# Where the FFT units stand in the slot list of a fused FFT filter and squared-ReLU feed-forward kernel

## The chip, the cores and the metric

The kernel runs on one core of one Trainium2 chip. The metric is device time in microseconds (us) of one execution. All times below come from the runs of the kernel before the change and from one profiled execution of it.

## What is computed

The input is x of shape 8 x 3008 x 256 (batch, sequence, channel). Along the sequence each channel goes through a real FFT, is multiplied by a complex filter and comes back through the inverse FFT. The result, read as 24064 rows of 256, goes through a feed-forward layer with a squared ReLU.

```python
X = np.fft.rfft(x, axis=1)
Y = X * (filt_r + 1j * filt_i)[None, :, :]
y = np.fft.irfft(Y, n=x.shape[1], axis=1)
h = np.maximum(y.reshape(24064, 256) @ w_in, 0.0)     # w_in 256 x 2048
out = h * h @ w_out                                   # w_out 2048 x 256
```

## The kernel before

**The feed-forward part sets the beat.** The rows are taken in 47 groups of 512. Each group has eight slots, so slot s belongs to group s // 8. In a slot TensorE (PE) makes two 128 x 512 blocks of h out of `yt` and the first weights (`ffn_g1`, L553). ScalarE (ACT) applies the ReLU (L557), and VectorE (DVE) squares the blocks of two slots at once (L564). One group later PE multiplies the squares with the second weights. For groups 0 to 5 and the last one that is `ffn_g2` (L573). For groups 6 to 45 it is `products` (L666), a scheme with seven products of half-size blocks instead of eight. That scheme needs four sums of h blocks (`sums`, DVE, L639 to L648) and adds on DVE (L681, L687) ahead of the stores (L604, L606) to `out`. The stores are issued by SyncE (SP). A `top` and a `bot` half are stored for each group, and the pool of their tiles has three buffers.

**The FFT part is cut into units that are strewn between.** The length 3008 is 64 x 47, and a batch goes through four stages:

- `load_x` (GpSimd's DMA queue, POOL) brings x, and `unit_a` (L358, 16 per batch) does the 47-point stage. ACT or DVE copies its result out of PSUM (L362, L364). After each four units `write_u` writes 384 KB to a DRAM tensor `dU`.
- `read_u` reads `dU` back in another order, with one 512 KB DMA and one 1024 KB DMA (L433), into the single buffer `ut`. `unit_b` (L442, 12 per batch) does the 64-point stage. DVE multiplies the result by the filter straight out of PSUM (L450), and two POOL DMAs add the two halves of the product to each other (L457). The products have five buffers. The first four units of a batch need the 512 KB part alone.
- `unit_p` (L487, 12 per batch) does the inverse 64-point stage on the finished product. ACT copies it out (L489), and after each three units 384 KB are written to `dZ` (L492).
- `read_z` reads a quarter of `dZ` with two 192 KB DMAs (L505) into one of two tiles `zt`, which the quarters use in turn. `unit_y` (L523, 16 per batch, four per quarter) does the inverse 47-point stage and ACT or DVE puts it into `yt` (L530, L532). `ffn_g1` reads `yt`. The first four units of a batch must be done before the group that holds the batch's first rows.

All units of the four kinds write to one PSUM tag with two buffers (`psF`). A unit can start when the copy out of the unit before the last has ended.

**The order is written out by hand.** Each engine works through its instructions in the order of the program, and so does SP's queue of DMA issues. `fft_plan(b)` (L690) gives each unit and each read of batch b a place counted in half-slots from a first slot `f` of the batch, which is 48 slots ahead of the group in which its rows begin (40 for batch 1). So batch b's list starts at slot 40, 88, 136, 184, 232 and 280 for b = 2 to 7. `run` (L729) executes what stands at a half-slot: place 0 comes right after the slot's `ffn_g1`, place 1 after its `products` or `ffn_g2`. The lists of all batches are merged into one dictionary, and nothing keeps two units out of the same half-slot. From f on, batch b still has its products to make while batch b + 1 has its `unit_a`. From f + 39 on, the first things of b + 1 and the `unit_y` of b stand among each other. This stretch, slots f + 38 to f + 55, is called the boundary of batch b in what follows.

Of the kernel before, what the change touches and what calls it, by code (L numbers as in the profile page):

```python
# [19 lines left out]
TG = 512  # L20
SLOTS = 8
# [89 lines left out]
def kernel(  # L111
# [9 lines left out]
    nc = tc.nc  # L121
    B, S, D = x.shape
# [564 lines left out]
                nc.vector.tensor_add(out=v, in0=o, in1=v)  # L687
                store(g, 0, 2, f["top"])

    def fft_plan(b):  # L690

        plan = {}

        def put(r, f, *a):
            r = int(2 * r)
            plan.setdefault(divmod(r, 2), []).append((f, a))

        d = 0
        if b == 1:
            for n in range(4, 16):  # L700
                put((n if n < 8 else n + 2 if n < 12 else 2 * n - 7) + n % 2 / 2, unit_y, 0, n)
            put(7.5, read_z, 0, 3)
            for k in range(4):
                put((4.5, 5.5, 7.5, 7.5)[k], cast_wout, k, nc.vector)
            for a in range(12, 16):
                put(2 + a / 2, unit_a, b, a)
            put(10.5, read_u, b)
            d = 7
        else:
            for a in range(16):  # L710
                if a % 2 == 0 and b > 2:
                    put((-57 + 2.3 * a) if b == 3 else (-66 + 2.75 * a), load_x, b, a // 2)
                put((-16 + a, -46 + 2.2 * a, -56 + 2.75 * a)[min(b, 4) - 2], unit_a, b, a)
            put(2 if b == 2 else -9, read_u, b)
        for p in range(12):
            r = 14 + 15 * p / 11 if b == 1 else 6 + 28 * p / 11 if b == 2 else -5 + 39 * p / 11
            put(r, unit_b, b, p)
            if b == 1 and 2 <= p < 10:
                put(r, load_x, 2, p - 2)
            put(r + 4.5, unit_p, b, p)  # L720
        for c in range(4):
            put((41, 41.5, 48, 54)[c] - d, read_z, b, c)
        for n in range(16):
            put(YN[n] - d, unit_y, b, n)
        return plan

    YN = (45, 45.5, 46, 46.5, 47.5, 49, 50.5, 52, 54, 56, 58, 60, 63, 66, 69, 72)

    def run(plan, r, place):  # L729
        for f, a in plan.get((r, place), ()):  # L730
            f(*a)


# [8 lines left out]
    for k in range(2):  # L742
        c = slice(12 * k, 12 * k + 12)
# [26 lines left out]
    for k in range(6):  # L770
        if k % 3 == 0:
            sSPx.append(p_u.tile([128, 12, 128], F16, tag="u", name=f"sSPx_{k}"))
        c, o = slice(4 * k, 4 * k + 4), slice(4 * k % 12, 4 * k % 12 + 4)
# [27 lines left out]
    read_z(0, 2)  # L801

    SEVEN = range(6, NG - 1)
    work = {}
    for b in range(1, B):
        first = (b * S // TG) * SLOTS - (48 if b > 1 else 40)
        for (r, place), w in fft_plan(b).items():
            work.setdefault((first + r, place), []).extend(w)

    for s in range((NG + 1) * SLOTS):  # L810
        g, k = divmod(s, SLOTS)
        if g < NG:
            ffn_g1(g, k)
        run(work, s, 0)
        if SEVEN[0] * SLOTS <= s < SEVEN[0] * SLOTS + 4:
            make_t(s % SLOTS)
        if (s - 1) // SLOTS - 1 in SEVEN:
            products((s - 1) // SLOTS - 1, (s - 1) % SLOTS)
        if g > 0 and g - 1 not in SEVEN:
            ffn_g2(g - 1, k)  # L820
        run(work, s, 1)
        if g > 0 and g - 1 not in SEVEN:
            ffn_out(g - 1, k)
        if g - 1 in SEVEN:
            sums(g - 1, k)
        if g < NG:
            ffn_sq(g, k)
# [30 lines left out]
```

## Time and profile before

| | |
|---|---|
| median of 14 runs | 788.09 us (785.9 to 790.35) |
| the profiled execution | 786.35 us, its span 784.2 us |
| TensorE busy | 754.8 us, 96% of the span, at full granted clock |
| VectorE busy | 619.7 us, 79% |
| ScalarE busy | 583.3 us, 74% |
| GpSimd busy | 192.7 us, 25% |
| DMA | 109.21 MB, mean 139 GB/s |

The page gives one execution. Busy time is the time in which an engine has an instruction in work. For TensorE the ends of matmuls are modelled, and a matmul is in work for longer than it keeps the next one from starting. A wait is put down to the line and the engine that ended it. An issue on SP's queue is not a transfer: the row tells when the DMA was handed over, not when it landed.

### The profile page before, as it was taken

The numbers are of one execution on the slowest core, as the hardware profiler recorded it, in microseconds if no ns is written. First come the engines' busy times: TensorE is split into PE (matmuls) and PEld (weight loads), VectorE is DVE, ScalarE is ACT, GpSimd is POOL, SyncE is SP. The second block draws the span as 40 slices with busy tenths as digits, with TensorE's granted clock in tenths as the row PEclk, the third lists the DMA queues.
The fourth block names the chain that finished last, engine by engine and source line by source line (L and its number), as shares of the span: only waits on it lengthen the run. The fifth ranks groups of instructions, "written<-read, shape, count | busy, mean of one in ns | idle before, by whom it ended". The sixth has DMA issues, their size and how long they took to land.

```text
span 784.2 us, 19161 instructions
## 1 busy us (share of the span) xinstructions
PE 754.8 (96%) x8022; PEld 553.2 (71%) x8022; DVE 619.7 (79%) x679; ACT 583.3 (74%) x831; POOL 192.7 (25%) x260
## 2 busy tenths in 40 slices
PE   8989989999989999999999999999998999999998
PEld 6746656667767777777768777687776877777776
DVE  5856654579778988888987899779987999878874
ACT  3976777778877887778877887778786777777774
POOL 3801650134213321222221323233311222000000
PEclk9999999999999999999999999999999999999999
DMA  9985896655775547665486554855536433421011
GB/s 364 373 252 159 151 169 190 168 105 116 148 195 127 108 99 183 165 129 99 106 217 131 113 125 97 207 128 116 103 87 193 121 69 80 112 70 55 28 50 60
DMA packets 104942, 109.21 MB, mean 139 GB/s; under 512 B 9640, under 2 KB 93096, under 8 KB 102936
## 3 DMA queue, kind: packets, MB, share of 16 engines
q1 hardware_dynamic: 85704, 87.38, 36.3%
q0 software_dynamic: 19008, 20.43, 19.6%
q8 instruction: 63, 1.03, 0.6%
q10 hardware_dynamic: 144, 0.18, 0.1%
q14 instruction: 23, 0.19, 0.1%
HBM read 58.12 MB, written 48.23 MB: 136 GB/s over the span
## 4 chain that ended last, share of the span: by engine, by line
PE 80%; DMA 9%; DVE 6%; ACT 2%; SPq 2%; issue 1%; DVEq 0%; ACTq 0%
PE psH L553 35%; PE psX L666 16%; PE psY L666 12%; PE psO L573 6%; DMA zt<-dZ 4%; DVE prod L450 3%; PE psA L358 3%; PE psP L487 2%; PE psY L523 2%; PE psB L442 2%; DMA f<-in_filt_i_dram 2%; DVE h L564 1%; DMA ut<-dU 1%; ACT h L557 1%; DMA wout<-in_moe_w_out_dram 1%
## 5 line engine op out<-in xcount | busy, mean ns | idle before, releaser
L557 ACT ACTIVATE h<-psH 128x1024 f16<-128x1024 f32 x376 | 384.6, 1024 | 156.6 <-PE psH L553 152.6
L553 PE MATMUL psH<-yt,sWin 128*128 128x512 f16 (+7 forms) x1728 | 386.7, 351 | 1.5 <-DVE yt L532 0.6
L564 DVE TENSOR_TENSOR h<-h 128x2048 f16<-128x2048 f16 (+1 forms) x192 | 229.8, 1197 | 68.5 <-ACT h L557 64.9
L457 POOL DMA_DIRECT2D prod<-prod x168 | 138.8, 972 | 462.3 <-DVE prod L450 456.4
L553 PEld LDWEIGHTS <-sWin 128*128 128x128 f16 x1728 | 152.8, 98 | 97.0 <-issue 3.8
L666 PEld LDWEIGHTS <-sum 128*128 128x128 f16 x2560 | 158.0, 98 | 25.2 <-issue 1.5
L666 PEld LDWEIGHTS <-h 128*128 128x128 f16 x1920 | 119.0, 98 | 20.5 <-issue 1.4
L450 DVE TENSOR_TENSOR prod<-psB,sF 128x1024 f16<-128x1024 f32 x84 | 102.5, 1220 | 26.6 <-PE psB L442 26.3
L666 PE MATMUL psX<-sT,sum 128*128 128x128 f16 x1280 | 91.0, 219 | 0.0
L666 PE MATMUL psY<-sT,sum 128*128 128x128 f16 x640 | 61.9, 219 | 0.0
L573 PE MATMUL psO<-sWout,h 128*128 128x256 f16 x448 | 56.9, 272 | 0.0
L523 PEld LDWEIGHTS <-zt 112*128 112x128 f16 x512 | 34.1, 98 | 29.2 <-issue 8.4
L532 DVE CAST yt<-psY 128x376 f16<-128x376 f32 x62 | 33.7, 544 | 26.1 <-PE psY L523 26.0
L362 ACT CAST u<-psA 96x512 f16<-96x512 f32 x90 | 52.3, 581 | 2.5 <-PE psA L358 1.9
L573 PEld LDWEIGHTS <-h 128*128 128x128 f16 x448 | 43.2, 98 | 14.8 <-issue 4.5
L489 ACT CAST ze<-psP 128x512 f16<-128x512 f32 x84 | 49.3, 587 | 4.1 <-PE psP L487 3.9
L523 PE MATMUL psY<-sC,zt 112*128 112x94 f16 x512 | 42.4, 205 | 9.5 <-DMA zt<-dZ 9.3
L642 DVE TENSOR_TENSOR sum<-sum,h 128x2048 f16<-128x2048 f16 x40 | 48.9, 1222 | 0.9
L666 PE MATMUL psY<-sWout,h 128*128 128x128 f16 x640 | 48.8, 219 | 0.0
L666 PE MATMUL psX<-sT,h 128*128 128x128 f16 x640 | 48.8, 219 | 0.0
L648 DVE TENSOR_TENSOR sum<-h,sum 128x2048 f16<-128x2048 f16 x40 | 48.6, 1216 | 0.0
L666 PE MATMUL psY<-sWout,sum 128*128 128x128 f16 x640 | 48.6, 219 | 0.0
(86 smaller groups left out, 706.1 us busy)
## 6 DMA issues: line engine op xcount, KB each, us to landing
zt<-dZ SPq DMA_DIRECT2D x64, 192.0 KB
dU<-u SPq DMA_DIRECT2D x28, 384.0 KB
prod<-prod POOLq DMA_DIRECT2D x168, 64.0 KB, 2.8
dZ<-ze SPq DMA_DIRECT2D x28, 384.0 KB
x<-in_x_dram POOLq DMA_DIRECT2D x40, 192.0 KB, 4.7
ut<-dU SPq DMA_DIRECT2D x7, 1024.0 KB
xw<-in_x_dram SPq DMA_DIRECT2D x6, 1024.0 KB
ut<-dU SPq DMA_DIRECT2D x7, 512.0 KB
```

The lines of the kernel that those rows point to most:

```text
L362: nc.scalar.copy(out=o, in_=pv)
L450: nc.vector.tensor_mul(out=prod, in0=ps.rearrange("p (a d) -> p a d", d=D).unsqueeze(1).to_broadcast([128, 2, 2, D]), in1=sF[:, :, 2 * p:2 ...
L457: nc.gpsimd.dma_start(out=prod[64 * i:64 * i + 64, 0], in_=prod[64 - 64 * i:128 - 64 * i, 1], accum_op=mybir.AluOpType.add)
L489: nc.scalar.copy(out=zes[(b, c)][:, 2 * i6:2 * i6 + 2, :], in_=ps.rearrange("p (a d) -> p a d", d=D))
L523: nc.tensor.matmul(ps[:, 94 * jj:94 * jj + 94], zt[:, 4 * (g % 2) + jj, dt * 128:(dt + 1) * 128], sSY, start=True, stop=True)
L553: nc.tensor.matmul(ps[:, i, o:o + n], sWin[:, dt, jt * 128:(jt + 1) * 128], yts[b][:, dt, r:r + n], start=(dt == 0), stop=(dt == 1))
L557: nc.scalar.activation(out=h2[:, 2 * s:2 * s + 2, :], in_=ps, func=AF.Relu)
L564: nc.vector.tensor_mul(out=v, in0=v, in1=v)
L573: nc.tensor.matmul(pso[g][:, t % 2, :], h2s[g][:, jt, t * 128:(t + 1) * 128], sWout[:, jt, :], start=(jt == 0), stop=(jt == NJT - 1))
L642: nc.vector.tensor_sub(out=t, in0=f[5], in1=a11)
L648: nc.vector.tensor_sub(out=t, in0=a12, in1=f[6])
L666: nc.tensor.matmul(o[:, t, :], f[p][:, q, 128 * t:128 * t + 128], sg["w"][p][:, q, :], start=(m == 0 and p in (1, 2)), stop=(q == 7), skip ...
```

## The change

Units no longer share half-slots. `fft_plan` now makes one list for all batches. Units of batch 1, and the first four `unit_y` of every batch, keep fixed places. All others have a wished place, and go, kind by kind (`unit_b`, `unit_p`, `unit_y`, `unit_a`), to the nearest half-slot that is still free. A half-slot with more than two of its four neighbours taken counts as two half-slots further away. Reads and loads are placed as before, and may share a half-slot with a unit.

Places that change, in slots after f:

- The first quarter of `dZ` is read at 40 instead of 41, and the second at 43 instead of 41.5. The reads of the third and fourth quarter stay at 48 and 54.
- `read_u` of the next batch goes from 9 to 6.5 slots ahead of that batch's f. For batches 3 to 7 that is from f + 39 of the batch before to f + 41.5: it was ahead of the first read of `dZ` and is now behind it. Batch 2's `read_u` stays where it is.
- The 12 `unit_b` of batches 3 to 7 go over 36 slots from -2 instead of 39 slots from -5.
- For batches 2 to 7 `unit_p` stands 7 slots behind its `unit_b` for the first one, falling to 4.5 for the last, instead of 4.5 throughout.
- `unit_y` 4 to 7 stand half a slot later (48, 49.5, 51, 52.5), and batch 3's `unit_a` are 2.1 slots apart instead of 2.2.

No instruction, DMA or tile is added or taken away. In the new list, units of batch 1 still share a half-slot with another unit at slots 19.5, 23.5 and 29.

```diff
-    def fft_plan(b):
-
-        plan = {}
-
-        def put(r, f, *a):
-            r = int(2 * r)
-            plan.setdefault(divmod(r, 2), []).append((f, a))
...
-                put((-16 + a, -46 + 2.2 * a, -56 + 2.75 * a)[min(b, 4) - 2], unit_a, b, a)
-            put(2 if b == 2 else -9, read_u, b)
-        for p in range(12):
-            r = 14 + 15 * p / 11 if b == 1 else 6 + 28 * p / 11 if b == 2 else -5 + 39 * p / 11
-            put(r, unit_b, b, p)
-            if b == 1 and 2 <= p < 10:
-                put(r, load_x, 2, p - 2)
-            put(r + 4.5, unit_p, b, p)
-        for c in range(4):
-            put((41, 41.5, 48, 54)[c] - d, read_z, b, c)
-        for n in range(16):
-            put(YN[n] - d, unit_y, b, n)
-        return plan
-
-    YN = (45, 45.5, 46, 46.5, 47.5, 49, 50.5, 52, 54, 56, 58, 60, 63, 66, 69, 72)
+    YN = (45, 45.5, 46, 46.5, 48, 49.5, 51, 52.5, 54, 56, 58, 60, 63, 66, 69, 72)
+
+    def fft_plan():
+
+        fixed, units, moves = [], [], []
+        for b in range(1, B):
+            f = (b * S // TG) * SLOTS - (48 if b > 1 else 40)
...
+                    units.append((f + (-16 + a, -46 + 2.1 * a, -56 + 2.75 * a)[min(b, 4) - 2],
+                                  unit_a, b, a))
+                moves.append((f + (2 if b == 2 else -6.5), read_u, b))
+            for p in range(12):
+                r = 14 + 15 * p / 11 if b == 1 else 6 + 28 * p / 11 if b == 2 else -2 + 36 * p / 11
+                (fixed if b == 1 else units).append((f + r, unit_b, b, p))
+                if b == 1 and 2 <= p < 10:
+                    moves.append((f + r, load_x, 2, p - 2))
+                (fixed if b == 1 else units).append((f + r + (4.5 if b == 1 else 7 - 2.5 * p / 11), unit_p, b, p))
+            for c in range(4):
+                moves.append((f + (40 + d / 7, 43, 48, 54)[c] - d, read_z, b, c))
+            for n in range(16):
+                (fixed if n < 4 else units).append((f + YN[n] - d, unit_y, b, n))
+        work, used, done = {}, set(), {}
+        for r, *u in fixed:
+            h = int(2 * r)
+            used.add(h)
+            work.setdefault(h, []).append(u)
+        rank = (unit_b, unit_p, unit_y, unit_a)
+        for r, *u in sorted(units, key=lambda u: (rank.index(u[1]), u[0])):
+            after = done.get((u[0], u[1]), -1)
+            h = min((h for h in range(max(int(2 * r) - 3, after + 1), int(2 * r) + 12)
+                     if h not in used),
+                    key=lambda h: (sum(h + i in used for i in (-2, -1, 1, 2)) > 2) * 2
+                    + abs(h - int(2 * r)))
+            used.add(h)
+            done[(u[0], u[1])] = h
+            work.setdefault(h, []).append(u)
+        for r, *u in moves:
+            work.setdefault(int(2 * r), []).append(u)
+        return work
+
+    def run(plan, s, place):
+        for f, *a in plan.get(2 * s + place, ()):
             f(*a)
...
-    work = {}
-    for b in range(1, B):
-        first = (b * S // TG) * SLOTS - (48 if b > 1 else 40)
-        for (r, place), w in fft_plan(b).items():
-            work.setdefault((first + r, place), []).extend(w)
+    work = fft_plan()
```

More of the change, by code (lines that the diff above doesn't have):

```diff
@@ L688, in products @@
                 store(g, 0, 2, f["top"])
-    def fft_plan(b):
-        plan = {}
-        def put(r, f, *a):
-            r = int(2 * r)
-            plan.setdefault(divmod(r, 2), []).append((f, a))
[L698 to L712, printed above, removed]
-                put((-16 + a, -46 + 2.2 * a, -56 + 2.75 * a)[min(b, 4) - 2], unit_a, b, a)
-            put(2 if b == 2 else -9, read_u, b)
-        for p in range(12):
-            r = 14 + 15 * p / 11 if b == 1 else 6 + 28 * p / 11 if b == 2 else -5 + 39 * p / 11
-            put(r, unit_b, b, p)
-            if b == 1 and 2 <= p < 10:
-                put(r, load_x, 2, p - 2)
-            put(r + 4.5, unit_p, b, p)
-        for c in range(4):
-            put((41, 41.5, 48, 54)[c] - d, read_z, b, c)
-        for n in range(16):
-            put(YN[n] - d, unit_y, b, n)
-        return plan
@@ L727 @@
-    YN = (45, 45.5, 46, 46.5, 47.5, 49, 50.5, 52, 54, 56, 58, 60, 63, 66, 69, 72)
-    def run(plan, r, place):
-        for f, a in plan.get((r, place), ()):
+    YN = (45, 45.5, 46, 46.5, 48, 49.5, 51, 52.5, 54, 56, 58, 60, 63, 66, 69, 72)
[3 more added lines that the diff above has]
+            f = (b * S // TG) * SLOTS - (48 if b > 1 else 40)
+            d = 0
+            if b == 1:
+                for n in range(4, 16):
+                    fixed.append(((n if n < 8 else n + 2 if n < 12 else 2 * n - 7) + n % 2 / 2,
+                                  unit_y, 0, n))
+                moves.append((7.5, read_z, 0, 3))
+                for k in range(4):
+                    moves.append(((4.5, 5.5, 7.5, 7.5)[k], cast_wout, k, nc.vector))
+                for a in range(12, 16):
+                    fixed.append((2 + a / 2, unit_a, b, a))
+                moves.append((10.5, read_u, b))
+                d = 7
+            else:
+                for a in range(16):
+                    if a % 2 == 0 and b > 2:
+                        moves.append((f + ((-57 + 2.3 * a) if b == 3 else (-66 + 2.75 * a)),
+                                      load_x, b, a // 2))
+                    units.append((f + (-16 + a, -46 + 2.1 * a, -56 + 2.75 * a)[min(b, 4) - 2],
[29 more added lines that the diff above has]
+        return work
```

## Prediction, made before the result was known

> **What bounds the kernel now.** I read the page first: the busy times, and the chain of work that ended last.
>
> ```profile
> PE 754.8 (96%) x8022; PEld 553.2 (71%) x8022; DVE 619.7 (79%) x679; ACT 583.3 (74%) x831; POOL 192.7 (25%) x260
> PE 80%; DMA 9%; DVE 6%; ACT 2%; SPq 2%; issue 1%; DVEq 0%; ACTq 0%
> ```
>
> PE is the bound, and no matmul leaves the program. All that can be won is PE's idle time and what is lost with it. So I cut the trace along the batches. The columns are the stretch, its length, and PE busy (instructions) first.
>
> ```profile
> 212.80:247.30 34.50, 31.54 (x380) 24.17 (x378) 27.22 (x30) 25.38 (x39) 7.70 (x10) 1.00 0.71 174
> 307.10:340.90 33.80, 31.58 (x380) 25.05 (x378) 27.23 (x30) 25.42 (x39) 7.71 (x10) 1.00 0.70 176
> 340.90:400.70 59.80, 59.80 (x653) 43.17 (x649) 52.35 (x56) 48.14 (x71) 16.42 (x22) 1.00 0.54 114
> 400.70:434.80 34.10, 31.58 (x380) 25.56 (x378) 27.22 (x30) 25.42 (x39) 7.70 (x10) 1.00 0.72 174
> 494.60:528.50 33.90, 31.57 (x380) 25.06 (x378) 27.22 (x30) 25.41 (x39) 8.93 (x12) 1.00 0.71 175
> 588.30:620.10 31.80, 29.75 (x373) 23.40 (x371) 27.06 (x30) 22.37 (x33) 6.57 (x8) 1.00 0.60 160
> ```
>
> Five short stretches, the boundaries of batches 2 to 6, lose 34.50 - 31.54 = 2.96, then 2.22, 2.52, 2.33 and 2.05 us: 12.1 in all. The long stretch between two of them loses nothing. It holds 32 slots, 1.87 us each. Then PE's waits, from 200 to 640 us and from 95 to 200 us; the columns are the sum, the number and the longest.
>
> ```profile
> PE psY L523 <- DMA zt<-dZ: 7.8, 5, 2.0
> PE psP L487 <- DVE prod L450: 2.4, 5, 0.5
> PE psA L358 <- DVE prod L450: 1.9, 8, 0.3
> ```
>
> ```profile
> PE psA L358 <- ACT ze L489: 1.5, 2, 1.2
> PE psA L358 <- ACT yt L530: 1.1, 1, 1.1
> PE psA L358 <- DVE prod L450: 0.8, 3, 0.3
> PE psA L358 <- DVE yt L532: 0.4, 1, 0.4
> PE psP L487 <- ACT u L362: 0.3, 1, 0.3
> PE psH L553 <- DVE yt L532: 0.2, 1, 0.2
> PE psY L523 <- ACT yt L530: 0.2, 1, 0.2
> ```
>
> The first three make up the 12.1 us. One kind is a late read of `dZ`, once per boundary. The other is a unit that finds both PSUM buffers still waiting to be copied out.
>
> A stall costs more than its idle time. These rows show why.
>
> ```profile
> 303.84 1.03 PE L553 MATMUL psH<-yt,sWin 128*128 128x512 f16 x4
> 307.99 0.38 PE L358 MATMUL psA<-x,sC 94*96 94x512 f16 x1
> 318.29 0.33 PE L523 MATMUL psY<-sC,zt 112*128 112x94 f16 x4 [1.26 <-DMA zt<-dZ]
> ```
>
> One 512-column matmul is in work for 0.38 us, but four take only 1.03, so they follow each other every (1.03 - 0.38) / 3 = 0.217, and a slot's four hold PE for 0.87. When PE stalls, 0.38 - 0.217 = 0.163 us of lost issue time still counts as busy. I add 0.163 per stall.
>
> **The crowding.** I set every unit of the old list beside PE's rows. A unit that stands at the same half-slot as the unit two before it, or one half-slot behind it, is where all the `psA`, `psP` stalls are. Of the units two or more half-slots apart, some 340, none stalls, the five waits for `zt` aside. In the new list, worked out from the diff's rule, only five units stand so close, all beside fixed units of batch 1 (slots 19.5, 21, 23.5, 24 and 29). So I count the cost of sharing as gone everywhere behind slot 29:
>
> - Boundaries: 2.4 + 1.9 idle in 13 stalls, 4.3 + 13 x 0.163 = 6.4 us.
> - From 95 to 200 us: the rows sum to 4.5 in 10 stalls. I keep 0.2 (`psH`, whose `unit_y` stays right ahead of its slot) and 0.3 of the 1.5 of `ACT ze`, where two units of batch 1 still share slot 29. 4.0 + 8 x 0.163 = 5.3 us.
>
> **The read of the first quarter.** Batch 3's boundary as an example: SP's queue, then one piece of the chain.
>
> ```profile
> 306.43 0.39 SPq L492 DMA_DIRECT2D dZ<-ze  x1
> 306.92 1.26 SPq L433 DMA_DIRECT2D ut<-dU  x2
> 308.28 1.56 SPq L606 DMA_DIRECT2D out_dram<-bot  x3
> 309.94 0.53 SPq L604 DMA_DIRECT2D out_dram<-top  x1
> ```
>
> ```profile
> 311.09 7.07 DMA zt<-dZ
> ```
>
> After that come two later issues of reads of `dZ`, and the row of SP's waits for them.
>
> ```profile
> 311.93 0.30 SPq L505 DMA_DIRECT2D zt<-dZ  x1
> 315.08 0.30 SPq L505 DMA_DIRECT2D zt<-dZ  x1
> ```
>
> ```profile
> SPq L505 <- DMA ut<-dU: 14.3, 7, 3.4
> ```
>
> The quarter's second half is handed over at 311.09 and lands 7.07 later, at 318.16; PE had been there since 318.29 - 1.26 = 317.0. Ahead of it in the queue stand the two reads of u, and the last row says that SP even holds back reads of `dZ` until reads of u land (311.93 and 315.08 here, so u's parts land 5.0 and 7.6 us after the issue). The Trainium skill (DMA: Bandwidth & Descriptors, Queues, rings and completion order) says that each DMA engine takes the descriptors of SP's queue in ring order; the 7.07 us behind u agree. By this rule the first quarter gains from its place and the second one pays for it, which is the first rival below.
>
> In the new order SP issues `dZ` write, `bot`, first quarter, `top`, u, second quarter. The quarter's second half needs the last `dZ` write landed. That wait is seen at batch 1, where no u stands between:
>
> ```profile
> 120.00 0.38 SPq L492 DMA_DIRECT2D dZ<-ze  x1
> 123.14 0.30 SPq L505 DMA_DIRECT2D zt<-dZ  x1
> ```
>
> The quarter's second half goes out 3.1 us after the write. For its landing I take the time that a transfer of the same size needs on another queue:
>
> ```profile
> x<-in_x_dram POOLq DMA_DIRECT2D x40, 192.0 KB, 4.7
> ```
>
> So here: 306.43 + 3.1 = 309.5, and landing after 4.7 at 314.3. PE comes at 317.0, so 2.7 us to spare. All five stalls go: 7.8 + 5 x 0.163 = 8.6 us.
>
> **What is late next.** Behind the waiting read SP holds `top` and u. `top`'s buffer comes up again only at the `bot` of the next group, six slots of 1.87 us on: covered; without that cover it would cost the 3.1 us per boundary. u follows `top` (0.53) at about 310.8 instead of 306.92 and lands in two parts at 315.8 and, by 7.6 from 311.3, at 318.9. The batch's first `unit_b` stands at f + 47, here slot 135, whose old start and the next one's are
>
> ```profile
> 321.73 0.38 PE L553 MATMUL psH<-yt,sWin 128*128 128x512 f16 x1
> 324.51 0.30 PE L553 MATMUL psH<-yt,sWin 128*128 128x320 f16 x1
> ```
>
> Less the stall won (1.4) and the `unit_b` moved away (0.2), and with the 0.87 of the slot's own matmuls ahead of it, PE gets there at 321.0: 5 us to spare. The second quarter now drains behind all of u. 318.16 is 3.1 behind u's second landing, so 318.9 + 3.1 = 322.0; `unit_y` 4 at slot 136 is reached at 324.51 - 1.4 - 0.6 (the crowding stall of slot 135) + 0.87 = 323.4. That is 1.4 us to spare, the thinnest margin of the change. The products need their POOL adds by `unit_p`, 4.5 to 7 slots on: 4.5 were enough before, since no row of PE waits for an add. Buffers of products: 7 slots behind at 3.3 slots apart is three or four in use, of five. Batch 2's u waits longer for its last `dU` write (`unit_a` 15 at 40.5 instead of 39, u at 42, first `unit_b` at 46): the 3.1 of such a write and u's 5.0 fit in four slots or fall short by tenths. POOL loads keep their places.
>
> **VectorE.** The first group of a batch gets three `unit_b` instead of two.
>
> ```profile
> 324.50:340.90 16.40, 15.91 (x205) 13.89 (x203) 13.26 (x15) 12.53 (x19) 5.48 (x7) 1.00 0.65 141
> 379.93 1.22 DVE L564 TENSOR_TENSOR h<-h 128x2048 f16<-128x2048 f16 x1
> 381.07 1.22 DVE L648 TENSOR_TENSOR sum<-h,sum 128x2048 f16<-128x2048 f16 x1
> ```
>
> DVE is the third number, 13.26 us. Its long operations start 1.14 apart, so 14.4 with one more, while PE without its two or three stalls there needs 16.40 - 0.49 - 0.4 = 15.5. DVE gets to 93%, not over.
>
> **The sum.** 8.6 + 6.4 + 5.3 = 20.3 us. Against it stands what the list newly brings: unbroken runs of units in neighbouring half-slots, more than twice as many as before, with DVE fuller. No row prices that. Below, it is nothing (units two half-slots apart never stalled). Above, it is the 6.4 of the old boundaries again. I take a stall of 0.2 + 0.163 at each of five boundaries, 1.8 us, nearer the lower end since that is the rule of the rows. Gain 18.5: 786.35 - 18.5 = 767.9 for the profiled execution. Its span is 784.2, so 2.1 lie around it. The median, 788.09, is 1.7 above it; the forecast for the median is 769.6.
>
> **Rivals.**
>
> 1. *The second quarter takes the place of the first.* It now stands behind both parts of u, and 1.4 us is little: if landing behind u is as late as the first quarter's was, PE waits at `unit_y` 4, and the 8.6 come back: 778. For it: 7.07 us for 192 KB. Against it: it is wanted three slots later than the first.
> 2. *The crowding comes back.* DVE at 93% in the first group makes copies out late, units two half-slots apart begin to stall, and the boundaries lose 6.4 instead of 1.8: 774. For it: a product's copy can sit behind two 1.14 us operations, longer than two half-slots, 1.87 us, less the matmul. Against it: the same pairs (two apart, DVE's copy before) are as many in the old list, and none cost anything.
> 3. *Slower: u comes too late for the next batch.* u is handed over 3.9 us later, and `unit_b` waits on PE ahead of everything else. To end slower than 788.09 by 0.2% (1.6), the five boundaries must lose 18.5 + 1.6 = 20.1, or 4.0 each. That needs u's first part at 321.0 + 4.0 = 325, 14.2 us after its issue instead of 5.0. At 15 us it would be 794. For it: u now shares the engines with the first quarter, `top` and the `dZ` write. Against it: all of these, u and the second quarter took 318.16 - 306.43 = 11.7 in the old order too.
> 4. *The change doesn't do what it says for `dZ`*: the quarter's lateness comes from the `dZ` write and not from u, and what is won in the crowding is eaten by PE then waiting for DVE. Then nothing remains, 787 to 789. The 14.3 us row and DVE's 52.35 of 59.80 us speak against it.
>
> **Chances.** Forecast 0.64; rival 2 0.16; rival 1 0.10; rival 3 0.05; rival 4 0.05. Some 0.2%, 1.6 us, is what a measurement of this kernel can tell from no change. Faster is the first three, 0.90; same 0.05; slower 0.05. The range holds the forecast and rival 2. Its lower end is the full 20.3 from the profiled execution, 766, less 0.5 for runs as they scatter: 765.5. Its upper end is rival 2 and a third of rival 1's 8.6: 774 + 3 = 777.
>
> **What would show it.** Right: PE's wait for `zt` at f + 45 is gone and the first quarter is handed over ahead of u; the five short stretches lose under 0.6 us each; `psA` and `psP` waits sum to under 2 us behind 115 us. Wrong: a wait of PE `psY` for `zt` at `unit_y` 4 (rival 1), `psA` or `psP` waits for DVE in the first group of each batch (rival 2), a wait of `psB` for `ut` (rival 3), or a `dZ` wait as long as before (rival 4).

## The result, and the profile after

| | before | after |
|---|---|---|
| median | 787.93 us (785.09 to 791.95, 47 runs) | 766.47 us (765.89 to 768.31, 10 runs) |
| the profiled execution | 786.35 us, span 784.2 | 766.38 us, span 764.6 |

The changed kernel takes 0.9732 of the time before (95% interval 0.9717 to 0.9747). It is faster, by 21.5 us in the medians and by 20.0 us in the profiled executions. The forecast was 769.6, in a range of 765.5 to 777: the sign and the mechanism held, the forecast was 3.1 us too high, and the time lies inside the range.

The page of the changed kernel, its busy times and the chain that ended last:

```profile
PE 750.9 (98%) x8022; PEld 552.5 (72%) x8022; DVE 620.1 (81%) x679; ACT 578.6 (76%) x831; POOL 192.4 (25%) x260
PE 88%; DVE 6%; DMA 3%; ACT 2%; issue 1%; POOL 0%; SPq 0%; ACTq 0%; DVEq 0%
```

In the chain PE went from 80% to 88% and DMA from 9% to 3%. PE's idle time was 784.2 - 754.8 = 29.4 us and is 764.6 - 750.9 = 13.7. Idle time fell by 15.7 and the span by 19.6. The 3.9 us between the two sit in PE's busy time, which fell although every matmul is still there. That is the share of a stall which the records count as busy: 3.9 / 0.163 is 24 stalls fewer, and the waits of PE from 58.9 to 784 us fell from 32 to 9.

The stretches of the changed kernel that hold the same slots as the five boundaries and the stretch between two of them (stretch, its length, then PE busy first; clock, DMA share and GB/s last):

```profile
238.00:298.50 60.50, 60.35 (x654) 43.52 (x653) 53.66 (x57) 48.57 (x73) 18.53 (x25) 1.00 0.57 118
298.50:328.90 30.40, 30.40 (x377) 24.56 (x375) 26.04 (x29) 24.19 (x37) 5.52 (x7) 1.00 0.69 185
571.10:600.10 29.00, 29.00 (x369) 23.03 (x367) 25.93 (x29) 21.10 (x31) 4.93 (x6) 1.00 0.65 174
```

PE has no idle time left at these boundaries, nor at the three others that the forecast counted. What is left of its waits between 58.9 and 784 us (the sum, the number, the longest):

```profile
PE psY L523 <- DMA zt<-dZ: 0.8, 1, 0.8
PE psP L487 <- DVE prod L450: 0.6, 2, 0.3
PE psH L553 <- DVE yt L532: 0.5, 2, 0.3
PE psY L523 <- DVE prod L450: 0.5, 3, 0.2
PE psB L442 <- ACT yt L530: 0.3, 1, 0.3
```

From 200 us on only the fourth row remains: `unit_y` 11 of a batch finds a buffer still waiting for the DVE product of the unit before the last, which stands two half-slots ahead (three times, of four such places). The first row is new. It is the first quarter of batch 1, whose read now stands behind a write of `dU`.

Batch 3's boundary, on SP's queue and on PE, in the changed kernel's timeline (start, duration, what):

```profile
297.82 0.39 SPq L492 DMA_DIRECT2D dZ<-ze  x1
299.36 1.69 SPq L606 DMA_DIRECT2D out_dram<-bot  x3
301.14 0.84 SPq L505 DMA_DIRECT2D zt<-dZ  x2
302.08 0.40 SPq L604 DMA_DIRECT2D out_dram<-top  x1
302.57 0.95 SPq L433 DMA_DIRECT2D ut<-dU  x2
303.58 1.03 SPq L505 DMA_DIRECT2D zt<-dZ  x2
...
308.26 0.33 PE L523 MATMUL psY<-sC,zt 112*128 112x94 f16 x4
...
312.35 0.38 PE L442 MATMUL psB<-ut,sSB 128*128 128x256 f16 x2
```

The order of issues is the forecast one. The quarter's second half goes out at 301.62, when the `dZ` write has landed, 3.8 us after that write was handed over (3.1 were counted). `unit_y` 0 starts at 308.26 and the first `unit_b` at 312.35, both with no wait.

### The profile page after: what moved, and what is told of

Its sections match the earlier page's. It is cut to its first block, busy times and chain, and to the rows that moved or that the text cites. A ratio compares the mean times of both kernels' runs of the same rounds, so it can differ in the third digit from the quotient of the medians.

```text
span 764.6 us, 19166 instructions
## 1 busy us (share of the span) xinstructions
PE 750.9 (98%) x8022; PEld 552.5 (72%) x8022; DVE 620.1 (81%) x679; ACT 578.6 (76%) x831; POOL 192.4 (25%) x260
## 4 chain that ended last, share of the span: by engine, by line
PE 88%; DVE 6%; DMA 3%; ACT 2%; issue 1%; POOL 0%; SPq 0%; ACTq 0%; DVEq 0%
PE psH L553 39%; PE psX L666 18%; PE psY L666 13%; PE psO L573 6%; PE psB L442 3%; PE psY L523 3%; PE psA L358 2%; PE psP L487 2%; DVE prod L450 2%; DVE h L564 1%; PE warm L272 1%; DMA zt<-dZ 1%; DMA wout<-in_moe_w_out_dram 1%; DMA dZ<-ze 1%; PE psf L291 1%
## 5 line engine op out<-in xcount | busy, mean ns | idle before, releaser
L666 PEld LDWEIGHTS <-h 128*128 128x128 f16 x1920 | 118.9, 98 | 19.5
L645 DVE TENSOR_TENSOR sum<-h 128x2048 f16<-128x2048 f16 x40 | 48.6, 1216 | 0.0
L639 DVE TENSOR_TENSOR sum<-h 128x2048 f16<-128x2048 f16 x40 | 48.6, 1215 | 0.0
```

Source lines behind the costliest of these rows:

```text
L639: nc.vector.tensor_add(out=t, in0=a21, in1=a22)
L645: nc.vector.tensor_sub(out=t, in0=a11, in1=a21)
L666: nc.tensor.matmul(o[:, t, :], f[p][:, q, 128 * t:128 * t + 128], sg["w"][p][:, q, :], start=(m == 0 and p in (1, 2)), stop=(q == 7), skip ...
```

## The experiments

Each ran beside the kernel before, whose median was 787.8 to 788.2 there. Each kernel says what it changes against the changed kernel, unless another is named.

**The list alone.** The old places, put through the new rule of one unit per half-slot.

```diff
-    YN = (45, 45.5, 46, 46.5, 48, 49.5, 51, 52.5, 54, 56, 58, 60, 63, 66, 69, 72)
+    YN = (45, 45.5, 46, 46.5, 47.5, 49, 50.5, 52, 54, 56, 58, 60, 63, 66, 69, 72)
...
-                    units.append((f + (-16 + a, -46 + 2.1 * a, -56 + 2.75 * a)[min(b, 4) - 2],
+                    units.append((f + (-16 + a, -46 + 2.2 * a, -56 + 2.75 * a)[min(b, 4) - 2],
...
-                moves.append((f + (2 if b == 2 else -6.5), read_u, b))
+                moves.append((f + (2 if b == 2 else -9), read_u, b))
...
-                r = 14 + 15 * p / 11 if b == 1 else 6 + 28 * p / 11 if b == 2 else -2 + 36 * p / 11
+                r = 14 + 15 * p / 11 if b == 1 else 6 + 28 * p / 11 if b == 2 else -5 + 39 * p / 11
...
-                (fixed if b == 1 else units).append((f + r + (4.5 if b == 1 else 7 - 2.5 * p / 11), unit_p, b, p))
+                (fixed if b == 1 else units).append((f + r + 4.5, unit_p, b, p))
...
-                moves.append((f + (40 + d / 7, 43, 48, 54)[c] - d, read_z, b, c))
+                moves.append((f + (41, 41.5, 48, 54)[c] - d, read_z, b, c))
```

> The new list, but with every read and every unit wished where the old plan had it (first quarters of dZ at 41 and 41.5, u at -9, products over 39 slots, unit_p 4.5 slots behind). Two separate terms (my theory): the crowding stalls are gone, and PE waits for zt once at each of the boundaries of batches 2 to 6 again, 1.2 to 2 us, so 8 to 10 us more than the changed kernel: 774 to 777. Rival, own half-slots do it all, since the reads are only late while units are crowded: 766 to 769 and no wait for zt over 0.8 us.

Measured 776.42 us (774.16 to 779.09, 4 runs), 0.9849 (0.9818 to 0.988) of before. PE's waits from 200 to 640 us, one row:

```profile
PE psY L523 <- DMA zt<-dZ: 8.4, 5, 3.1
```

From 200 us on the crowding is gone, and the late quarter is untouched, as the first theory had it. The list is worth 787.8 - 776.4 = 11.4 us; the forecast for the crowding was 6.4 + 5.3 = 11.7.

**The places alone.** The kernel before, with its old dictionaries and nothing that keeps two units apart, but with every wished place of the changed kernel. This edit is against the kernel before.

```diff
-                put((-16 + a, -46 + 2.2 * a, -56 + 2.75 * a)[min(b, 4) - 2], unit_a, b, a)
-            put(2 if b == 2 else -9, read_u, b)
+                put((-16 + a, -46 + 2.1 * a, -56 + 2.75 * a)[min(b, 4) - 2], unit_a, b, a)
+            put(2 if b == 2 else -6.5, read_u, b)
...
-            r = 14 + 15 * p / 11 if b == 1 else 6 + 28 * p / 11 if b == 2 else -5 + 39 * p / 11
+            r = 14 + 15 * p / 11 if b == 1 else 6 + 28 * p / 11 if b == 2 else -2 + 36 * p / 11
...
-            put(r + 4.5, unit_p, b, p)
+            put(r + (4.5 if b == 1 else 7 - 2.5 * p / 11), unit_p, b, p)
...
-            put((41, 41.5, 48, 54)[c] - d, read_z, b, c)
+            put((40 + d / 7, 43, 48, 54)[c] - d, read_z, b, c)
...
-    YN = (45, 45.5, 46, 46.5, 47.5, 49, 50.5, 52, 54, 56, 58, 60, 63, 66, 69, 72)
+    YN = (45, 45.5, 46, 46.5, 48, 49.5, 51, 52.5, 54, 56, 58, 60, 63, 66, 69, 72)
```

> The old merging without the list, so that units share half-slots, but every wished place of the new plan (first quarter ahead of u, products over 36 slots, unit_p 7 slots behind). Two separate terms: no wait for zt at the boundaries of batches 2 to 6, and psA, psP, psY or psB waits wherever a unit stands at most one half-slot behind the unit two before it. There are 63 such units here and 45 in the kernel before, where they cost 11.7 us, so some 16 us: 778 to 784. Rival, the order of the reads does it all: 766 to 770.

Measured 784.82 us (784.46 to 786.35, 7 runs), 0.9963 (0.9949 to 0.9978), 0.8 above what was expected. PE's waits in this kernel from 200 to 640 us:

```profile
PE psA L358 <- ACT ze L489: 6.1, 8, 1.2
PE psY L523 <- ACT yt L530: 2.1, 5, 0.4
...
```

No row for `zt`, but more crowding than before, above all at four slots (102, 150, 198, 246) where three units now share a half-slot. The two parts don't simply add: the places bring 3.0 alone and 9.9 on top of the list. In the 11.4 + 9.9 = 21.3 of both nothing is missing.

**u read first.** In the changed kernel only the read of u goes back ahead of the first quarter.

```diff
-                moves.append((f + (2 if b == 2 else -6.5), read_u, b))
+                moves.append((f + (2 if b == 2 else -9), read_u, b))
```

> The changed kernel with one number back: u is read 9 slots ahead of its batch instead of 6.5, so ahead of the first quarter of dZ. All units stand as in the changed kernel. My theory: the first quarter drains behind u again, PE waits for zt 1 to 2 us at five boundaries, 774 to 777, and the single runs scatter as widely as those of the kernel before (some 5 us instead of 2.4). Rival, the quarter's place in slots (40 instead of 41) or the wait for the dZ write matters and not u: 766 to 769.

Measured 769.87 us (769.42 to 772.16, 4 runs), 0.977 (0.9747 to 0.9794). Neither theory: the order costs 3.4 us, not the 8 to 10 of the one and not nothing. The expected scatter of some 5 us did not come either, it is 2.7. PE's waits for `zt` in it, 200 to 640 us:

```profile
PE psY L523 <- DMA zt<-dZ: 2.5, 3, 0.9
```

**The first two quarters' reads at their new places, and nothing else.** So the list alone was run again with the new places of `read_z`: the first quarter goes from 41 to 40 and the second from 41.5 to 43. u stays ahead of both, products and `unit_p` stay old. The edit is against the list alone.

```diff
-                moves.append((f + (41, 41.5, 48, 54)[c] - d, read_z, b, c))
+                moves.append((f + (40 + d / 7, 43, 48, 54)[c] - d, read_z, b, c))
```

> The new list with the old places, and only the reads of the first two quarters at their new ones (40 and 43 slots, so ahead of top); u stays ahead of them at -9, products over 39 slots from -5, unit_p 4.5 slots behind. If the quarter's place ahead of top is worth what list_only and u_first differ by (776.4 against 769.9), and the shift of the products is worth nothing by itself: 769 to 771, waits for zt of some 3.5 us in all. Rival, the later products and unit_p of u_first also took load off the DMA engines at that point: 772 to 776.

Measured 768.64 us (767.42 to 769.45, 4 runs), 0.9757 (0.9723 to 0.9791), a little below the expected 769 to 771, with 1.2 us of waits for `zt` instead of some 3.5. PE's waits, 200 to 640 us:

```profile
PE psY L523 <- DMA zt<-dZ: 1.2, 2, 0.6
PE psP L487 <- DMA prod<-prod: 0.3, 1, 0.3
```

Of the 9.9 us that the places bring on top of the list, 776.4 - 768.6 = 7.8 come from this one line. The second quarter's new place changes little in the order of SP's queue: at batch 3 it stands next behind the first quarter in the list alone and next behind `top` with the new places. So what the line changes there is the order of `top` and the first quarter, but no run moves the second quarter by itself. What the first quarter's place does is seen on SP's queue at batch 3's boundary, in the list alone and in the kernel with u first, where the first quarter again stands at slot 40:

```profile
301.51 0.39 SPq L492 DMA_DIRECT2D dZ<-ze  x1
...
304.84 0.54 SPq L604 DMA_DIRECT2D out_dram<-top  x1
305.42 2.09 SPq L505 DMA_DIRECT2D zt<-dZ  x3
```

```profile
298.63 0.39 SPq L492 DMA_DIRECT2D dZ<-ze  x1
...
302.36 1.12 SPq L505 DMA_DIRECT2D zt<-dZ  x2
303.53 0.48 SPq L604 DMA_DIRECT2D out_dram<-top  x1
```

And the pieces of the chains of waits of the same two kernels, in the same order (start of the hand-over, time to landing):

```profile
306.16 7.10 DMA zt<-dZ
```

```profile
302.93 6.39 DMA zt<-dZ
```

Counted from the `dZ` write the quarter lands after 306.16 + 7.10 - 301.51 = 11.75 us at slot 41, behind `top`, and after 302.93 + 6.39 - 298.63 = 10.69 at slot 40, ahead of it. That is 1.06 us, and the average stall to be removed was 8.4 / 5 = 1.7.

At batch 2 the place does more. `top` goes out in three issues there, and in the list alone SP holds back both halves of the first quarter behind them, until the two parts of u have landed. The second half, as a piece of the chain:

```profile
217.18 4.30 DMA zt<-dZ
```

PE waits 3.1 us, the longest of its five waits. With the new places both halves go out ahead of `top`, with no such wait, and PE waits 0.6 us:

```profile
213.15 1.19 SPq L505 DMA_DIRECT2D zt<-dZ  x2
```

Counted along SP's issues, the halves that are held back at batch 2 are the eighth behind the part of u for which they wait; ahead of `top` they are the fifth. The same holds for every wait of a read of `dZ` for u from 170 to 640 us: all seven in the kernel before, six in the list alone and five with the new places stand eight issues behind the part of u that they wait for.

**The first quarter a slot later, behind no u.** The other side of the same question: the changed kernel with the quarter back at 41.

```diff
-                moves.append((f + (40 + d / 7, 43, 48, 54)[c] - d, read_z, b, c))
+                moves.append((f + (41, 43, 48, 54)[c] - d, read_z, b, c))
```

> The changed kernel with the first quarter of dZ read at 41 slots instead of 40: behind the store of top, as before, but still ahead of u (41.5). If being ahead of u is what counts, the quarter is handed over half a microsecond to one later, PE has some 2 us to spare, and nothing changes: 766 to 768, no wait for zt at the boundaries of batches 2 to 6. Rival, the place ahead of top is worth as much as the one ahead of u (with u ahead of the quarter but top behind it PE lost only 3.4 us): waits for zt of 0.3 us or more at these boundaries, 768 to 771.

Measured 766.99 us (766.63 to 767.53, 4 runs), 0.9743 (0.9725 to 0.9761), as the first theory had it. From 200 to 640 us there is one wait for `zt`, of 0.2 us, and it is one for the second quarter (`unit_y` 4 of batch 6):

```profile
PE psY L523 <- DMA zt<-dZ: 0.2, 1, 0.2
```

Ahead of u the first quarter's slot hardly matters. The stall had two cures, place and order, and the change has both. The order alone comes within 0.5 us of the changed kernel; the place alone, with u ahead, leaves 2.2 (the run above) to 3.4 (u read first).

**The products over 39 slots again**, while u is read behind the quarter. `unit_p`, which is placed from its product, moves with them.

```diff
-                r = 14 + 15 * p / 11 if b == 1 else 6 + 28 * p / 11 if b == 2 else -2 + 36 * p / 11
+                r = 14 + 15 * p / 11 if b == 1 else 6 + 28 * p / 11 if b == 2 else -5 + 39 * p / 11
```

> The changed kernel with the products over 39 slots from -5 again, u still read behind the first quarter. u's first part lands 5 to 6 us after it is handed over (302.6 in the profile of the changed kernel), at about 308; PE gets to the batch's first unit_b, four slots earlier than in the changed kernel, at about 305.5. My theory: PE waits for u 2 to 3 us at each of five boundaries, and where such a wait makes the granted clock fall it loses 1.7 us more: 780 to 790, near the kernel before. Rival, u's read has slack enough, and the 36 slots are worth nothing: 766 to 769.

Measured 787.95 us (783.98 to 790.8, 10 runs), 0.9998 (0.9978 to 1.0017): the whole gain is gone, as the first theory had it. PE's only row from 200 to 640 us:

```profile
PE psB L442 <- DMA ut<-dU: 16.4, 5, 3.8
```

**`unit_p` 4.5 slots behind its product throughout.**

```diff
-                (fixed if b == 1 else units).append((f + r + (4.5 if b == 1 else 7 - 2.5 * p / 11), unit_p, b, p))
+                (fixed if b == 1 else units).append((f + r + 4.5, unit_p, b, p))
```

> The changed kernel with unit_p 4.5 slots behind its unit_b in all batches, as before. My theory: the seven slots are worth nothing, since 4.5 slots were enough for the products' adds: 766 to 768, no psP waits for adds. Rival, the adds land late behind the other DMAs and PE waits for the first products of each batch: psP waits of 0.3 us or more in each of six batches, 769 to 773.

Measured 784.6 us (781.74 to 785.82, 6 runs), 0.9943 (0.992 to 0.9966). Here the theory on record fell: the seven slots are worth 18.1 us. PE's waits, 200 to 640 us, then one of them on the timeline with the adds that it waited for and what SP hands over beside them:

```profile
PE psP L487 <- DMA prod<-prod: 9.3, 4, 2.5
PE psP L487 <- DVE sum L645: 2.9, 1, 2.9
PE psP L487 <- DVE prod L450: 1.5, 5, 0.6
```

```profile
319.09 1.69 POOL L457 DMA_DIRECT2D prod<-prod  x2 [19.49 <-DVE prod L450]
319.15 0.41 SPq L341 DMA_DIRECT2D dU<-u  x1
319.66 2.06 SPq L505 DMA_DIRECT2D zt<-dZ  x2
321.81 1.30 SPq L606 DMA_DIRECT2D out_dram<-top  x3
...
326.86 0.38 PE L487 MATMUL psP<-prod,sSP 128*128 128x256 f16 x2 [2.92 <-DVE sum L645]
```

PE stands still for 2.92 us and goes on 7.8 us after the adds were begun to be handed over. The row names DVE as the releaser, but by its place and length it is the fifth wait of the first row's kind, for the adds: all five stand at the first `unit_p` of a batch, 1.9 to 2.9 us each. The adds are in flight together with a 384 KB write of `dU`, the read of the third quarter and stores.

**The third quarter later, in that kernel.** The edit is against the kernel with `unit_p` 4.5 slots behind. If the quarter's 384 KB are what delays the adds, reading it 2.5 slots later frees them.

```diff
-                moves.append((f + (40 + d / 7, 43, 48, 54)[c] - d, read_z, b, c))
+                moves.append((f + (40 + d / 7, 43, 50.5, 54)[c] - d, read_z, b, c))
```

> p_early (unit_p 4.5 slots behind its unit_b throughout) with the read of the third quarter of dZ at 50.5 slots instead of 48, behind the adds of the first products instead of among them. If these adds land late because the third quarter's 384 KB and the store of top are handed over around them, the waits of psP for adds shrink from 2.5 to 2.9 us per boundary to under 1 us, the clock stays, and the time is 767 to 773. Rival, the adds take 5 to 7 us there whatever else is moved: 780 or more, as p_early.

Measured 773.24 us (773.16 to 775.58, 4 runs), 0.9828 (0.9796 to 0.9859), just above what was expected. The waits for adds, 200 to 640 us:

```profile
PE psP L487 <- DMA prod<-prod: 5.2, 4, 1.7
```

The direction was right, the size not: waits under 1 us were expected. 9.3 + 2.9 became 5.2, so the quarter's read is somewhat over half of it. What else delays the adds there stays open; the `dU` write and the stores of the timeline above are candidates, and no run moved them.

**Half of the seven slots.**

```diff
-                (fixed if b == 1 else units).append((f + r + (4.5 if b == 1 else 7 - 2.5 * p / 11), unit_p, b, p))
+                (fixed if b == 1 else units).append((f + r + (4.5 if b == 1 else 5.75 - 1.25 * p / 11), unit_p, b, p))
```

> The changed kernel with unit_p 5.75 slots behind its unit_b for the first product, falling to 4.5, half way between p_early and the changed kernel. If the adds land late by a fixed time, the waits of 2.5 to 2.9 us per boundary of p_early become 0.1 to 0.6 us, too short for the clock to fall: 766 to 770. Rival, p_early lost its time because unit_p and unit_b crowd each other, and the place in the list matters: 772 or more, with psP waits for copies and not for adds.

Measured 772.27 us (771.94 to 773.59, 4 runs), 0.9815 (0.9792 to 0.9838). The adds' waits shrank to one row, but others came (200 to 640 us):

```profile
PE psY L523 <- DVE prod L450: 1.5, 4, 0.4
PE psP L487 <- DVE yt L532: 1.4, 4, 0.4
PE psP L487 <- DMA prod<-prod: 0.8, 1, 0.8
```

The first row is `unit_y` 11, two half-slots behind a `unit_b`, and the second is `unit_p` 5, three half-slots behind a `unit_y` that DVE copies; both come four times, with 0.35 to 0.4 us each. Two single waits of 0.6 and 0.2 us, put down to ACT, stand at the first `unit_p` of a batch like the third row, so they are probably waits for adds too. The rival named the time that came, 772, but its cause does not hold for the kernel with 4.5 slots, where PE waited for adds. Moving `unit_p` moves the whole list, so the distance that the adds need can't be read from this run without the list's own cost.

**What was left, mended.** Batch 1 and the last `unit_y` of batch 0 enter the list too, so that no two units share a half-slot any more (slot 21 was a fourth place where they still did); batch 1's first quarter is read half a slot earlier, so that the `dU` write stands behind it; two `unit_a` of batch 2 get fixed half-slots ahead of it; `unit_y` 11 moves by half a slot.

```diff
-    YN = (45, 45.5, 46, 46.5, 48, 49.5, 51, 52.5, 54, 56, 58, 60, 63, 66, 69, 72)
+    YN = (45, 45.5, 46, 46.5, 48, 49.5, 51, 52.5, 54, 56, 58, 60.5, 63, 66, 69, 72)
...
-                    fixed.append(((n if n < 8 else n + 2 if n < 12 else 2 * n - 7) + n % 2 / 2,
-                                  unit_y, 0, n))
+                    (fixed if n < 8 else units).append(
+                        ((n if n < 8 else n + 2 if n < 12 else 2 * n - 7) + n % 2 / 2, unit_y, 0, n))
...
-                    units.append((f + (-16 + a, -46 + 2.1 * a, -56 + 2.75 * a)[min(b, 4) - 2],
-                                  unit_a, b, a))
+                    (fixed if b == 2 and a > 13 else units).append(
+                        (f + (-16 + a if a < 14 else a / 2 - 7, -46 + 2.1 * a,
+                              -56 + 2.75 * a)[min(b, 4) - 2], unit_a, b, a))
...
-                (fixed if b == 1 else units).append((f + r, unit_b, b, p))
+                units.append((f + r, unit_b, b, p))
...
-                (fixed if b == 1 else units).append((f + r + (4.5 if b == 1 else 7 - 2.5 * p / 11), unit_p, b, p))
+                units.append((f + r + (4.5 if b == 1 else 7 - 2.5 * p / 11), unit_p, b, p))
...
-                moves.append((f + (40 + d / 7, 43, 48, 54)[c] - d, read_z, b, c))
+                moves.append((f + (40.5 if b == 1 else 40, 43, 48, 54)[c] - d, read_z, b, c))
```

> The changed kernel with batch 1's units in the list too, batch 1's first quarter read half a slot earlier (ahead of a write of dU that now lands before it), and unit_y 11 half a slot later. The waits that are left in the changed kernel are psY for zt 0.8, psP for prod 0.6 in two, psY for prod 0.5 in three, psB for yt 0.3: 2.2 us in 7 or 8 stalls, and 0.163 each: some 3.4 us less, 762 to 765. Rival, the waits only move to the next unit: 766 to 767.

Measured 762.43 us (762.27 to 762.57, 4 runs), 0.9685 (0.9667 to 0.9702) of before, 4.0 us under the changed kernel and faster than both. Of the five rows of waits one is left, from 58.9 to 784 us:

```profile
PE psH L553 <- DVE yt L532: 0.5, 2, 0.3
```

The idle time that went is 0.8 + 0.6 + 0.5 + 0.3 = 2.2 us in 7 stalls; with 7 x 0.163 hidden that makes 3.3 of the 764.6 - 760.8 = 3.8 us of span.

## Why the prediction was right, and where it was wrong

**The bound and the kind of the gain: right.** PE's idle time was all that could be won, and 15.7 us of it went, together with 3.9 that PE's busy time had hidden.

**The crowding: right in size.** 11.7 were counted, and 1.8 of new stalls against them, 9.9 in all. The list alone brought 11.4 in the medians, and 786.35 - 775.53 = 10.8 in the profiled executions, for which the terms were counted.

**Right in size, half wrong in cause: the read of the first quarter.** 8.6 were counted; the places bring 9.9 on top of the list in the medians and 775.53 - 766.38 = 9.2 in the profiled executions. But the step "Ahead of it in the queue stand the two reads of u" gave the whole lateness to u. With u left ahead, a place one slot earlier takes the waits from 8.4 to 1.2 us, and with u put back ahead in the changed kernel only 3.4 us are lost. The quarter's own place behind `top` was as much a cause.

The boundary that was taken as the example also hid a second way of being late. At batch 3 the reads that SP held back until u landed, at 311.93 and 315.08, were the second quarter's. At batch 2 of the kernel before they were the first quarter's own, and the chain of waits runs through them (start, time to landing):

```profile
213.16 8.20 DMA ut<-dU
221.38 3.21 DMA zt<-dZ
```

So that stall, the longest of the five, was a late hand-over and not a slow transfer. At the other boundaries SP's waits cost PE little: in the list alone SP held back reads of `dZ` until u landed for 12.6 us in six waits, with the quarters' new places still for 9.1 in five, while PE's waits all but vanished.

```profile
SPq L505 <- DMA ut<-dU: 12.6, 6, 2.7
```

A long wait of the queue's own need not be one that PE waits for. In the changed kernel, where u stands behind the first quarter, SP no longer waits for u there at all.

Against the forecast's second view, the ring order in the queue, nothing speaks: the order alone is worth the 3.4 us. No run separates the transfer from what stands ahead of it, but the boundaries can be compared. Handed over when u has landed, the 192 KB take 3.21 us (4.30 in the list alone); behind u in the queue they take 7.07. And it need not be u: at batch 1 of the changed kernel, behind a write of `dU`, they take 6.58.

```profile
119.44 6.58 DMA zt<-dZ
```

**The price of the list: right, with another rule.** 1.8 us were allowed for new stalls; the new ones are 0.8 at batch 1 and 0.5 in the three waits at `unit_y` 11, with 0.163 for each 2.0. The lower end, however, rested on "units two half-slots apart never stalled", and that falls. `unit_y` 11 stalls for 0.5 / 3 = 0.17 at just that distance, and with half of the seven slots units two and even three half-slots behind stall 0.4 each. Rival 2 did not come, but not because the distance is safe. In the changed kernel's list 32 units stand two half-slots behind a `unit_b`, 33 in the list before, and of the 32 only `unit_y` 11 waits; what else decides, no run separates. DVE itself, at 26.04 of 30.40 us in a boundary and 13.91 of 15.41 in the first group of batch 3 (14.4 of 15.5 were counted), did not become the bound.

**Wrong: "4.5 were enough before, since no row of PE waits for an add".** That was read from an order in which u and the products stood elsewhere. In the new order the adds meet the read of the third quarter, and 4.5 slots cost 18.1 us. Here the forecast was lucky: it came out only because the change has the seven slots, and the reason for them was missing.

**Rival 3 named the right danger.** u comes later, and with products from -5 on PE waits 16.4 us for it, which together with the clock (the last section) loses the whole gain. It did not come because the first `unit_b` was moved as well: it starts 312.35 - 302.57 = 9.8 us after u is handed over, 321.0 - 310.8 = 10.2 were counted, and it does not wait. In the kernel with products from -5, u's first part lands 5.0 to 6.2 us after it is handed over (5.0 were counted), so by this estimate some 4 us were to spare. The second quarter, forecast as the thinnest margin (rival 1), made no stall.

**Mis-sized: the 1.7 us from the profiled execution to the median.** "The median, 788.09, is 1.7 above it" was carried over to the kernel after, where the profiled execution is the median (766.38 and 766.47). Without that term the forecast would have been 767.9, 1.4 from the measured time. That rest is the two terms above, 10.8 against 9.9 and 9.2 against 8.6.

What the 1.7 is, the granted clock of the single executions shows. 32 executions of the kernel before, those beside the experiments, have it on record. The nine with a mean clock of 0.999 or 1.000 took 784.8 to 786.8 us, the seventeen with 0.997 or 0.998 took 787.2 to 789.3, and the six with 0.995 or 0.996 took 788.4 to 790.1. The profiled execution had 1.000. One step of half clock, as the last section shows it, makes 0.5 x 3.41 / 785 = 0.0022 of the mean clock and 1.7 us of time. So the median of the kernel before seems to hold one such step that its profiled execution lacks. Of ten executions of the changed kernel seven had 1.000 (765.9 to 766.7 us) and three 0.997 or 0.998 (768.1 to 768.3); the mended kernel's four all had 1.000, and scatter by 0.3. That PE's waits bring such steps about is seen in the profiles of two other kernels (last section), and is argued for the kernel before.

## What to carry to other kernels

A read that is moved in a queue moves its readers' and its neighbours' margins, and the parts of such a move belong together: two parts of this one, left out singly, cost 18.1 and 21.5 us, nearly the whole gain, while another part alone (the new places of the first two quarters' reads, on top of the list) had most of it and needed neither. So try the smallest move that takes a read ahead of one issue, before an order of reads is turned round. With two PSUM buffers, give each unit a half-slot of its own and count on small stalls up to three half-slots behind a slow copy. Count the issues of a queue too: a read that stands far enough behind a large one may be handed over only when that one has landed. A margin read from the old order ("nobody waits") is only good for the old order.

## What the runs showed of the hardware

**A stall of PE can cost twice.** In the profiled executions of two kernels the granted clock fell to a half after stalls of PE behind 200 us, each time for one step of 3.41 us, which costs 1.7. Rows of the kernel with `unit_p` 4.5 slots behind (stretch, its length, PE busy, clock, DMA share, GB/s):

```profile
419.99:423.40 3.41, 1.37 (x16) 1.00 1.03 198
423.40:426.81 3.41, 3.41 (x25) 0.50 0.05 10
```

And one of the kernel with the products over 39 slots:

```profile
216.98:220.39 3.41, 1.42 (x18) 1.00 0.96 317
```

The changes of the clock in one execution lie on a grid of 3.41 us, and the share of one step in which PE is idle is what seems to count, not the length of the stall. From 200 us on, the steps of these two kernels that were followed by half a clock, three and four of them, were idle for at least 1 - 1.37 / 3.41 = 0.60 of the step (the one at 419.99); the one at 216.98, idle for 0.58, was not, although PE waited 3.6 us there, over two steps. In the list alone a wait of 3.1 us, longer than any of the kernel with `unit_p` 4.5 slots behind (2.9), straddled two steps too:

```profile
219.78:223.19 3.41, 1.57 (x28) 1.00 1.01 168
```

That is 0.54 idle, and the clock stayed. The number isn't a law, though: in the start phase of the list with the two quarters' new places, a step with 0.45 idle was followed by half a clock too, and so was one in that of the kernel with the products over 39 slots.

```profile
46.14:49.55 3.41, 1.89 (x27) 1.00 0.99 300
49.55:52.96 3.41, 3.41 (x9) 0.50 1.07 266
```

The Trainium skill (TensorE: Matmul & The Clock Gate, Part 1) gives a free-running window of about 3.4 us and half the clock after an idle one. The window and the half agree; that the window need not be idle throughout is what these rows add. The clock explains most of what the waits leave open: with `unit_p` 4.5 behind, 13.7 us of waits and 3 x 1.7 make 18.8 of the 784.0 - 764.6 = 19.4 us of span; with the products over 39 slots 16.4 and 4 x 1.7 make 23.2 of 24.4, and the step in its start phase is a fifth.
